# Cross attention and a gated feed-forward on one core: half-height score products for batch 1, whole-row stores of the state tokens, and a redrawn instruction order

## The chip, the cores and the metric

The kernel runs on 1 core of one Trainium2 chip. The metric is the device time of the program in microseconds (us). Three timed executions of the kernel before lie between 647.27 and 648.13 us, with a median of 647.93 us.

## The reference

There are B = 8 batches, H = 8 heads, S = 512 tokens and Ns = 32 state tokens of D = 64 elements per head. Tokens read the states and states read the tokens; all 8 x (512 + 32) result rows of 512 elements then go through a gated feed-forward with d_ff = 1536.

```python
scale = 1.0 / np.sqrt(D)
a = softmax(scale * x @ state.T)          # [B, H, 512, 32]
xread = a @ state                         # [B, H, 512, 64]
a2 = softmax(scale * state @ x.T)         # [B, H, 32, 512]
sread = a2 @ x                            # [B, H, 32, 64]
t = concatenate([xread, sread], axis=2)   # rows of 512 = all heads
out = ((t @ w_a) * (t @ w_b)) @ w_out
```

(The reference's softmax adds 1e-9 to its sum; it is written out there.)

## The kernel before

**Two parts per number.** Every fp32 operand of the large products is split into a rounded part and a remainder (names ending in `_h` and `_l`), and each product is three matmuls: h·h, l·h and h·l. ScalarE (ACT) makes the rounded part by a copy, VectorE (DVE) subtracts to get the remainder, and TensorE (PE) multiplies.

**Stages.** For tokens, `a @ state @ w_a` is computed as `a @ (state @ w_a)`: the small product of states and weights comes first, either directly (`Batch.direct0`, `Batch.direct`, lines 773 to 801) or by way of a scratch tensor in memory (`project`, `Batch.load`). `layer1` (line 922) multiplies it with the transposed attention weights `at_h`, `at_l` into the banks `ab`, and `layer2` (line 951) or `term` (line 1231, a scheme of seven products for pairs of batches) multiplies with the output weights into the banks `acc`. Finished token tiles are transposed by DVE and stored (`Batch.give`). The 8 x 32 state rows go last, as a unit of their own (`States`, line 859; `states2`, line 962): their sums stand in two `ms` banks, i = 0 and i = 1, of 128 rows each.

**Scores.** Batches 0 and 1 come first (`attend`, line 1010). `Attention.scores` (line 616) makes the scores of one batch and one of two groups g of four heads. The input holds two heads side by side over 64 rows each, and the states are stored with zeros in the rows of the other head, so a product runs over all 128 rows (64 of them zeros) into 32 output rows: 4 products per group, 8 per batch. Batches 2 to 7 use another function, `scores` (line 545), with 64 rows of contraction, in which heads of both groups alternate. For batch 1 the scores are kept by two ACT copies (`keep`, line 633), transposed by PE (`turned`), reduced, exponentiated and normed by DVE and ACT, transposed back and split into `at_h`, `at_l`.

**The end.** In the last call of `states2`, tile i = 0 is copied out of its bank by ACT (`States.close`, line 904) and stored by two DMAs (`States.give`, line 910), one per half of the columns h. Tile i = 1 is copied before its last matmuls, which go into two fresh banks of 256 columns; DVE adds each of these to the copy and each half is stored by its own DMA. A half is not contiguous in a row of the output: it is 4 pieces of 64 elements (256 bytes) in each of 128 rows.

**Order.** All calls are first recorded as units (one instruction, or several that belong together), and then issued in the order of a written-out list, `ORDER` (line 142). Each engine works through its own units in that order, and so does the queue of SyncE (SP), which issues every DMA. The list has 4896 units: 2556 of PE, 1035 of DVE, 734 of ACT and 571 of SP.

Of the kernel before, what the change touches and what calls it, by code (L numbers as in the profile page):

```python
# [14 lines left out]
ALU = mybir.AluOpType  # L15
# [4 lines left out]
P = 128  # L20
# [122 lines left out]
6 40-42 1 12-13 54 7 3 0 23 14 43-45 55 46-48 56 28 49 8-9 2 15 68 24 50 29 10 4 57 25-26 58 115 16 30 59 51 31 60 33  # L143
17 61 52 75 20 18 69 34 114 21 116 62-63 37 82 38 53 35 22 64 712 70 77 381 538 117 65 530 66 202 19 83 118-120 67 71
714 36 84 88 212 217 299 85-86 72 89 87 121 128 122 94 90 207 123 91 73 92-93 104-106 129 95 107 124 130 96 125 108
131 382 98 132 99 126 222 100 133 158 127 134 97 39 101-102 76 213 78 214 164 161-162 165 109 103 135 167 166 110 159
136 111 215 139 137 142 140 79 204 366 168 376 138 141 300 163 148-149 554 203 702 150-151 143 563 144-145 713 209 112
160 205 80 223 152 146 208 153 539 147 186 194 190 169 187 113 371 198 191 219 722 154-155 170 210 199 218 195 224 171
156 715 386 176 172 229 220 196 173 236 200 177 157 178 174 197 201 179 225 692 378 260 239 175 704 237 180 192 368
181 263 555 182 247 562 248 377 240 564 264 367 238 188 703 540 383 393 301 211 183 241 249 732 546 242 250 369 384 27  # L150
717 243 716 251 244 189 245-246 266 304 302 265 267 252-253 261-262 705 32 184 373 388 724 607 254 275-278 269 723 270
379 305 271 279 372 193 185 272 280 291 531 273 374 541 556 274 303 387 257 281 268 255 400 297 230 375 258 231 292
226 259 403 306 282 307 389 707 293 725 334 395 335 401 308 390 328 309 916 310 74 404 402 311 547 604 336 391 288 565
608 289 698 285 232 318 283 312 733 337 256 718 294 726 708 727 313 338-339 548 314 566 227 346 568 295 569 315 233
316 585 405 693 317 606 329 406 330 290 319 570 298 296 407 234 408-409 411 532 5 412 325 358 410 331 587 286-287 824
533 326 417 586 385 332 719 605 720 577 284 567 709 340 359 734 341 413 342 588 414 343-344 327 590 415 578 735 416
360 571 589 345 721 814 572 81 461-462 354 380 322-323 464 737 347 324 418 728 463 333 350 433-434 534 394 465 362 351
435 596 436 579 437 355 729 557 439 396 438 710 597 609 363-364 320 440 361 321 348 598 580 445 441 352 356 365 424
442 466 694 558 549 467 706 421 443-444 419 695 425 357 353 528 430 730 629 422 468 599 469 610 581 446 472 559 535
699 470 630 397 631 582 426 634 420 473 349 427 452 474 423 428 431 471 432 453 475 573 478 612 429 476 449 632 494  # L160
611 834 550 583 206 542 600 455 711 477 529 495 615 479 748 458 731 456 744-745 459 496 450 497 613 447 460 454 451
221 398 491 536 633 498 614 500 457 482 816 483 480 649 484-485 640 501 551 746 749 448 742 492 502 648 503 601 486
621 602 543 743 747 488 493 552 739 622 499 510-511 641 487 504 804 740 603 522 228 1224 906 506 1225 741 505 514 1227
523 1243 584 560 399 524 481 489 507 512 515 490 1226 1228 759 508 758 513 1244 696 518 1245 642 736 697 1229 519 235
516 700 1230 1246 520 1247 517 525 635 1200 825 1248 1257 664 1255 643 1231 760 544 1232 1260 1233 1201 1258 561 1202
11 1203 521 644 1204 738 1205 1249 1194 1261 826 623 1234 1250 553 1218 526 665 1195 624 1197 1241 1235-1236 509 625
1237 756 537 1214 1251-1253 757 1259 1238 626 645 216 761 627 1219 1254 1239 768 1256 545 1240 797 666 1215 1242 769
646 754 370 936 1196 805 1198 1262 1199 628 1216 651 1263 765 815 667 527 755 647 1268 1264 668 827 1375 1220 1376 616
1210 650 836 750 817 1265 751-752 669 652 753 764 1206 806 1207 1266 1269-1271 766 1267 767 1211 1272-1273 1208 1274
658 1290 1209 1282-1283 1399 1284 670 1377 671 1275-1277 1221 762 1278-1279 1285 1293 653 1217 1294 1286 807 1280 1291  # L170
1281 1287 772 1379 763 1288 1295 1292 818 1289 679 835 809 770 654 1296 701 591 1297-1298 673 907 1299 672 1301 1300
392 1302 773 1223 1303 771 828 819 1304-1305 837 1400 1440 829 1382 1307 1306 1323 1308 926 1212 1315 820 574 808 1380
1316 1309 674 659 656 1310-1311 831 1312-1314 918 1317 1442 1324 1318-1319 1213 832 821 1326 1401 1445 1320-1321
1334-1335 782 1383 811 838 1325 1322 1327 1336-1337 830 1328 833 1446 784 927 1329 1378 783 675 1330-1333 822 1356
1443 1222 1340 678 1338 799 655 812 1357 917 1339 1441 1342 1358 839 1384 1343 1444 660 1344 810 1345 1359 1341 1447
774 1348 661 1480 1349 1346 841 1350 1347 813 1499 1351 1462 775 919 1352 1354 785 1467 1353 846 1361-1362 1409 1360
1464 1363 847 842 938 937 778 676 592 780 1402 662 1364 1355 939 1406 908 840 677 1365 686 781 1367 1381 663 1368 1366
657 928 844 1410 779 1483 680 1369 1373 1562 909 786 1503 1370 776 845 1371-1372 777 1385 681 788 1421 843 687 1374
1391-1392 789 911 688 1386 1403 1387 1407 1422 1393 1388 910 1394 823 1389 1404 912 1395 1390 1396 1468 1481 1512 1423
# [3 lines left out]
1565 1439 1476 894 1451 1472 1500 1454 862 1419 858 1477 691 1455-1456 1452 873 1453 1471 865 793 859 1415 1554 1457  # L183
1420 876 1478 1460 1458-1459 1479 860 878 921 1504 1485 1416 1486 1556 1473 1487-1488 879 1501 1461 874 893 1509 1489
1474 1491-1492 1490 877 922-923 1566 1581 1475 1557 948 1493 861 1494 1497 900 1505 875 1495-1496 1506 1525 1539 884
1517 1510 866 1555 932 1498 1502 1559 1526 1679 1511 946 1531-1532 933 684 885 1558 1564 994 867 1514 895 940 1527
1533 1528 924 1522 1534 1507 1529 864 934 1540 1680 1530 1523 1560 925 1561 1583 949 1518 863 888 943 1508 996 947
1543 1775 1582 935 1584 995 1537 1519 794 950 1524 1520 1535-1536 1521 1544 1567-1568 1622 1538 951-952 1585 795 889
997 1569 956 953 962 954 1570-1573 963 1152 1613 1574-1576 944 964 1603 998 1546 1586 1605 796 1587 965 1542 1625 901
1547 1588 945 1579 1714 801 1604 1606 1545 942 999 1623 1645 1577-1578 1580 1548 1589 1550 1590 1655 1591-1593 1609  # L190
1594-1597 1610 802 1598 1551 1715 955 1552 1614 1601 1549 1599 1626 1600 880 957 1001 1656 1627 1616 803 1000 1628
1624 1611 1541 1553 881 896 1602 960 1619 1615 1617 1739 967 1633 1612 902 1153 1629 882 887 1634 636 1607 1630 961
1620-1621 1631 897 1154 1632 1608 886 1155 1635 1166 1636 1647 1618 1738 958 1681 1651 1648 1637 1654 903 1639 1652
# [3 lines left out]
1812 1694 1708 1702-1703 1157 1704-1705 1744 1720 1745 1712 1709 1724-1725 1710 1726 1717 1004 1660 1168 1756 982 1711  # L197
1741 1727 973 1005 1776 1169 1713 980 1175 1742 1757 1730 1162 1728 1731 1759 1891 1787 1006 1732 1729 1746 1733 1736
1159 1743 1721 1786 1718 1163 1851 1835 1760 1758 1761 983 1894 1753 1734 1754 1762 1719 1735 1737 1763 891 1722
# [160 lines left out]
def attn_moe(ctx, tc, xt, xn, sd, wl, w_out, out):  # L360
# [238 lines left out]
    class Attention:  # L599
# [776 lines left out]
```

## Time and profile before

| what | value |
|---|---|
| median of 3 timed runs | 647.93 us |
| the profiled execution's own time | 650.51 us |
| its span (first to last instruction) | 648.7 us |
| PE, DVE, ACT busy share of the span | 98%, 86%, 63% |
| granted TensorE clock, mean over the span | 0.995 |
| memory read, written | 119.80 MB, 55.05 MB |

The profiled execution is 2.58 us over the median of the timed runs; 1.8 us of its own time lie outside the span. Busy time of PE includes the pipelining of matmuls, so a busy share of 98% says that there was always a matmul under way, not that they followed each other at the smallest distance.

### The profile page before, as it was taken

Reading aid. Unit: us, or ns where it says so; the run is one execution under the profiler, and the core shown is the slowest. Engines: PE = TensorE matmul, PEld = TensorE weight load, DVE = VectorE, ACT = ScalarE, POOL = GpSimd, SP = SyncE. Lnnn points to the kernel's source line nnn. Section 1 sums busy time; section 2 is a strip of 40 time slices with the busy share of each in tenths; the row PEclk is TensorE's granted clock in tenths of the full one; section 3 lists DMA queues with packets and bytes.
Section 4 is the critical chain, followed back from the end, with each engine's and each line's share of the span. In section 5 each row is a group of like instructions: output and inputs, shape, how many; then the busy total and the mean of one; then the engine's idle time right before and its main releaser. Section 6 shows DMA issues by size and latency. Waiting matters only on the chain.

```text
span 648.7 us, 10343 instructions
## 1 busy us (share of the span) xinstructions
PE 636.4 (98%) x3554; PEld 496.8 (77%) x3554; DVE 557.4 (86%) x1035; ACT 407.2 (63%) x751; POOL 0.7 (0%) x6
## 2 busy tenths in 40 slices
PE   7999999999999999999999999999999999999996
PEld 4666777667887887786878886888788888888885
DVE  4799999998996898999998999999976887476785
ACT  3889886799994667657666765664443834544331
POOL 0000000000000000000000000000000000000000
PEclk9899999999999999999999999999999999999999
DMA  8998888999699989999979789977998366387706
GB/s 308 311 405 275 277 275 284 355 303 368 223 340 316 335 306 326 303 343 260 307 273 352 238 285 358 302 253 218 292 294 246 104 198 216 97 264 218 232 1 162
DMA packets 145380, 175.54 MB, mean 271 GB/s; under 512 B 48048, under 2 KB 102832, under 8 KB 145328
## 3 DMA queue, kind: packets, MB, share of 16 engines
q1 hardware_dynamic: 145328, 174.89, 82.6%
q8 instruction: 28, 0.46, 0.3%
q14 instruction: 24, 0.20, 0.1%
HBM read 119.80 MB, written 55.05 MB: 270 GB/s over the span
## 4 chain that ended last, share of the span: by engine, by line
PE 78%; DVE 11%; ACT 4%; DMA 4%; issue 2%; SPq 0%; DVEq 0%; POOLq 0%; POOL 0%; ACTq 0%
PE ab L1333 38%; PE acc L1333 30%; PE ms L1333 10%; DMA wt<-s_dram 2%; DVE kept_g L1333 2%; DVE g_l L1333 1%; DMA p_raw<-scr 1%; DVE stg L1333 1%; DVE s_p L1333 1%; DVE m L1333 1%; DVE p_l L1333 1%; DVE a_tr L1333 1%; DVE xst L1333 1%; ACT wq L1333 1%; DMA scr<-sw 1%
## 5 line engine op out<-in xcount | busy, mean ns | idle before, releaser
L1333 PE MATMUL acc<-g_h,wt 128*128 128x512 f32 x588 | 203.8, 392 | 0.5 <-DMA wt<-s_dram 0.5
L1333 PE MATMUL ab<-at_h,p_h 128*128 128x512 f32 x384 | 148.1, 398 | 2.3 <-ACT a_sb L1333 1.5
L1333 ACT COPY a_sb<-ab 128x512 f32<-128x512 f32 (+1 forms) x120 | 67.9, 566 | 130.9 <-PE ab L1333 120.3
L1333 PE MATMUL ab<-at_l,p_h 128*128 128x512 f32 x384 | 146.8, 391 | 0.1
L1333 PE MATMUL ab<-at_h,p_l 128*128 128x512 f32 x384 | 145.0, 392 | 0.0
L1333 PEld LDWEIGHTS acc<-g_h,wt 128*128 128x128 f32 x588 | 109.8, 188 | 27.3 <-issue 3.4
L1333 PE MATMUL acc<-g_l,wt 128*128 128x512 f32 x294 | 108.5, 390 | 0.0
L1333 PEld LDWEIGHTS ab<-at_h,p_h 128*128 128x128 f32 x384 | 72.2, 188 | 27.7 <-ACT a_sb L1333 7.5
L1333 ACT CAST g_h<-kept_g 128x512 fp32r<-128x512 f32 x126 | 76.8, 622 | 20.8 <-DVE kept_g L1333 11.2
L1333 DVE TENSOR_TENSOR g_l<-kept_g,g_h 128x512 fp32r<-128x512 f32 x126 | 84.3, 681 | 5.6 <-PE acc L1333 2.8
L1333 DVE TENSOR_TENSOR kept_g<-ab,a_sb 128x512 f32<-128x512 f32 x84 | 57.6, 686 | 32.5 <-PE ab L1333 25.3
L1333 PEld LDWEIGHTS ab<-at_h,p_l 128*128 128x128 f32 x384 | 72.1, 188 | 16.6 <-issue 1.7
L1333 PEld LDWEIGHTS ab<-at_l,p_h 128*128 128x128 f32 x384 | 72.1, 188 | 15.1 <-DVE at_l L1333 0.5
L1333 PEld LDWEIGHTS acc<-g_l,wt 128*128 128x128 f32 x294 | 55.2, 188 | 11.2
L1333 DVE TENSOR_TENSOR stg<-acc,stg 128x512 f32<-128x512 f32 x82 | 55.4, 683 | 7.2 <-PE acc L1333 5.3
L1333 ACT CAST p_h<-p_raw 128x512 fp32r<-128x512 f32 x72 | 44.3, 621 | 12.4 <-DMA p_raw<-scr 11.3
L1333 DVE TENSOR_TENSOR p_l<-p_raw,p_h 128x512 fp32r<-128x512 f32 x72 | 48.4, 680 | 3.7 <-ACT p_h L1333 3.7
L1333 PE MATMUL ab<-xs,sw_st 128*128 128x512 f32 (+1 forms) x192 | 51.1, 337 | 0.4 <-ACT a_sb L1333 0.4
L1333 ACT COPY sw<-ms 128x512 f32<-128x512 f32 x72 | 41.4, 589 | 11.4 <-PE ms L1333 10.9
L1333 PEld LDWEIGHTS ab<-xs,sw_st 128*128 128x128 f32 x192 | 34.5, 188 | 7.7 <-ACT a_sb L1333 1.2
L1333 PE MATMUL acc<-g_h,wo 128*128 128x512 f32 x96 | 33.3, 396 | 0.0
L1333 DVE TENSOR_TENSOR kept_g<-kept_g 128x512 f32<-128x512 f32 x42 | 28.4, 679 | 0.1
(130 smaller groups left out, 817.9 us busy)
## 6 DMA issues: line engine op xcount, KB each, us to landing
wt<-s_dram SPq DMA_DIRECT2D x42, 512.0 KB, 6.1
scr<-sw SPq DMA_DIRECT2D x72, 256.0 KB, 5.3
p_raw<-scr SPq DMA_DIRECT2D x36, 512.0 KB, 5.8
wt<-wo_dram SPq DMA_DIRECT2D x63, 256.0 KB, 5.0
raw<-wl SPq DMA_DIRECT2D x24, 512.0 KB, 7.1
x_in<-f_dram SPq DMA_DIRECT2D x36, 256.0 KB, 4.5
out<-turned SPq DMA_DIRECT2D x64, 128.0 KB, 4.4
xn<-xn SPq DMA_DIRECT2D x16, 512.0 KB, 5.3
```

The costliest lines, as they stand in the source:

```text
L1333: getattr(obj, method)(*map(real, args), **{k: real(x) for k, x in kw.items()})
```

## The change

Three things change.

1. Batch 1's scores: the 8 products of 128 rows become 8 products of 64 rows, with the heads of the two groups alternating. They stay one unit of the list.
2. States' output: each of the two tiles is stored by one DMA of 128 rows of 2,048 contiguous bytes, where there were two of 512 pieces of 256 bytes each. For tile i = 1 the DMA comes after both additions. The program has two units fewer (4894), both of them DMAs.
3. The list `ORDER`: all of its 200 lines are replaced. The first seven PE units are the same; after them the order differs on every engine, from beginning to end.

```diff
         def scores(self, psp, tag):
...
             self.raw = kept[self.b][:, self.g]
+            if self.b:
+                return
             with rec.together():
                 self.unread(0, self.s)
...
+        def product(self, hp, hh):
+            n = at(self.g, 2 * hp + hh) * NS
+            nc.tensor.matmul(self.s[n:n + NS], lhsT=self.st[ROWS[hh], hp, hh * NS:(hh + 1) * NS], rhs=self.x[ROWS[hh], hp], start=True, stop=True)
...
-        def give(self, i, h, ps=None):
-            o = self.sums[:, i].rearrange("p (j k x) -> p j k x", j=4, x=32)[:, :, 2 * h:2 * h + 2]
-            if ps is not None:
-                v = o.rearrange("p j k x -> p k j x")
-                nc.vector.tensor_tensor(out=v, in0=ps.rearrange("p (k j x) -> p k j x", k=2, x=32), in1=v, op=ALU.add)
+        def add(self, i, h, ps):
+            v = self.sums[:, i].rearrange("p (j k x) -> p k j x", j=4, x=32)[:, 2 * h:2 * h + 2]
+            nc.vector.tensor_tensor(out=v, in0=ps.rearrange("p (k j x) -> p k j x", k=2, x=32), in1=v, op=ALU.add)
+
+        def give(self, i):
             r = B * S + i * P
-            nc.sync.dma_start(out=out[r:r + P].rearrange("p (j k x) -> p j k x", j=4, x=32)[:, :, 2 * h:2 * h + 2].rearrange("p j k x -> p j (k x)"),
-                              in_=o.rearrange("p j k x -> p j (k x)"))
+            nc.sync.dma_start(out=out[r:r + P], in_=self.sums[:, i])
...
                 if last and i:
-                    u.give(i, h, ps)
-            if last and not i:
-                u.close(i)
-                for h in range(2):
-                    u.give(i, h)
+                    u.add(i, h, ps)
+            if last:
+                if not i:
+                    u.close(i)
+                u.give(i)
...
             for a in gs:
                 a.load()
+            for a in gs:
+                a.scores(*ms)
             with rec.together():
-                for a in gs:
-                    a.scores(*ms)
+                for hp in range(2):
+                    for a in gs:
+                        for hh in range(2):
+                            a.product(hp, hh)
```

Of the list, the two lines before and after in which the scores of batch 1 stand (117 is their unit; 118 and 119 are the two ACT copies, 120 the PE transposes; 39 and 72 are ACT casts, 21 and 83 to 85 PE products, 73 and 546 DVE units):

```diff
-17 61 52 75 20 18 69 34 114 21 116 62-63 37 82 38 53 35 22 64 712 70 77 381 538 117 65 530 66 202 19 83 118-120 67 71
-714 36 84 88 212 217 299 85-86 72 89 87 121 128 122 94 90 207 123 91 73 92-93 104-106 129 95 107 124 130 96 125 108
...
+59 70 33 60 115 20 114 61 116 34 217 300 18 52 37 82 702 53 62 83 63 19 38 77 530 212 35 64 69 202 65 71 117 538 39
+84-85 21 72 66 118-119 371 73 67 120 546 88 121 128 86 207 22 87 122 89 36 90 712 222 94 376 129 76 91-93 104-105 123
```

## Rows read from the trace of the kernel before

**Rows 1.** The page: busy time and share by engine, then the chain by engine.

```profile
PE 636.4 (98%) x3554; PEld 496.8 (77%) x3554; DVE 557.4 (86%) x1035; ACT 407.2 (63%) x751; POOL 0.7 (0%) x6
...
PE 78%; DVE 11%; ACT 4%; DMA 4%; issue 2%; SPq 0%; DVEq 0%; POOLq 0%; POOL 0%; ACTq 0%
```

**Rows 2.** Windows: stretch; length, busy PE, PEld, DVE, ACT, POOL; clock; DMA; GB/s.

```profile
60.00:120.00 60.00, 59.91 (x345) 44.41 (x345) 58.78 (x121) 45.65 (x84) 0.00 (x0) 1.00 0.86 290
120.00:200.00 80.00, 79.68 (x378) 61.33 (x378) 70.61 (x131) 70.80 (x128) 0.00 (x0) 1.00 0.91 317
200.00:320.00 120.00, 118.02 (x535) 93.52 (x534) 109.29 (x195) 81.85 (x150) 0.00 (x0) 1.00 0.96 311
320.00:400.00 80.00, 79.55 (x595) 63.73 (x594) 75.34 (x138) 51.27 (x93) 0.00 (x0) 1.00 0.88 298
400.00:500.00 100.00, 99.60 (x690) 79.63 (x690) 89.91 (x173) 51.02 (x97) 0.00 (x0) 1.00 0.89 269
```

**Rows 3.** Chain, 21 to 26 us and at 58.8 us: start, length, work.

```profile
21.93 1.85 PE ms L1333 x16
...
24.45 0.87 PE ms L1333 x8
...
58.76 1.02 PE ms L1333 x16
```

**Rows 4.** Timeline, ACT, 21.9 to 26 us: start, length, instruction, [idle before].

```profile
21.96 0.59 ACT L1333 CAST at_h<-ab 128x512 fp32r<-128x512 f32 x1 [0.73 <-PE ab L1333]
...
22.99 0.59 ACT L1333 COPY kept<-ms 128x512 f32<-128x512 f32 x1
23.85 0.59 ACT L1333 COPY kept<-ms 128x512 f32<-128x512 f32 x1 [0.28 <-PE ms L1333]
...
25.29 0.64 ACT L1333 CAST wo<-t 128x512 fp32r<-128x512 f32 x1
```

**Rows 5.** Timeline, DVE, 22 to 27 us.

```profile
22.55 0.47 DVE L1333 TENSOR_SCALAR t<-raw 128x512 int32<-128x512 uint32 x1 [1.23 <-DMA raw<-wl]
24.92 1.29 DVE L1333 TENSOR_REDUCE m<-ms 128x16 f32<-128x512 f32 x2 [1.91 <-PE ms L1333]
...
26.72 0.68 DVE L1333 TENSOR_TENSOR wo<-t,wo 128x512 fp32r<-128x512 f32 x1
```

**Rows 6.** Timeline, PE: batch 1's scores (21.86 us on), batch 2's (58.69 us on).

```profile
21.86 1.06 PE L1333 MATMUL ms<-x_raw 128*32 128x512 f32 x8
22.74 1.04 PE L1333 MATMUL ms<-xg 128*32 128x512 f32 x8
...
58.69 0.62 PE L1333 MATMUL ms<-x_raw 64*32 64x512 f32 x2
...
58.73 0.62 PE L1333 MATMUL ms<-x_nat,s_p 64*32 64x512 f32 x2
59.14 0.60 PE L1333 MATMUL ms<-x_raw 64*32 64x512 f32 x2
```

**Rows 7.** Timeline, the end: the last DMA issues (SPq), last matmul, additions (DVE).

```profile
643.02 2.65 SPq L1333 DMA_DIRECT2D out<-sums  x4
...
643.48 0.28 PE L1333 MATMUL acc<-wo_st,g_l 128*128 128x256 f32 x1
643.70 0.75 DVE L1333 TENSOR_TENSOR sums<-acc,sums 128x256 f32<-128x256 f32 x2 [2.10 <-ACT sums L1333]
...
645.09 0.58 SPq L1333 DMA_DIRECT2D out<-sums  x1
```

**Rows 8.** Page, DMA issues: count, KB each, median us from issue to landing.

```profile
out<-sums SPq DMA_DIRECT2D x4, 128.0 KB, 2.2
```

**Rows 9.** Tile x_raw, only its first DMA (576 KB, at 0.7 us).

```profile
L1333 SPq DMA_DIRECT2D x_raw<-xt x1: 406/406/406, 0.7 to 0.7; - x1
...
DMA to landing us min/median/max: 3.5/3.5/3.5
```

**Rows 10.** Chain, its longest wait for a DMA: start, length, work.

```profile
192.61 7.94 DMA p_raw<-scr
```

More of the change, by code (lines that the diff above doesn't have):

```diff
@@ L148 @@
[L148 to L152, printed above, removed]
@@ new lines @@
+2033 2091 1032 2306 2083 1027 2307 2081 2062 2578 2084 2096 2067 2097 2063 2059 2085 2125 2585 2094 2086 2088 2064
+2239 2072 1029 2111 2240 2087 2060 1050 2098 1060 2061 2308 2210 2103 2285 2100 2202 2104 2112 2089 1035 2117 2260
+1033 2201 2099 2259 2068-2070 1042 2073 2118 1061 2286 2203 1049 2113 2119 2074 2114 2309 1030 2071 1058 2101 2115
+2167 1040 2168 2075 2238 2120 2116 2294 2426 2121 1043 1041 2123 2204 2122 2128 2124 2438 2102 1028 1051 2205 2187
+2129 2105 2169-2170 2188-2189 2131 1031 2406 2148 2429 2178 2171 2179 2132 2193-2194 2172 1048 2190 1068 2195 2133
@@ new lines @@
+2337 2398 2342 2399 2343 2403 2344 2166 2186 2507 1086 1067 2417 2345 2432 2400 2411-2412 2435 2257 2353 2433 2413
+2434 2418 1070 2404 2371 2354 2401 2480 2419 2444 2414 2436 2445 1087 2370 2437 2448 2420 2415 2446 2508 2481 2449
+2482 2176 2421 2483 2447 2571 2405 2416 2485 1088 2422 2361 2465 2486 2484 2423 2457 1075 2372 2569 2362 2374 2450
+1084 2424 2509 2529 2154 2175 2363 2183 1076 2373 1077 2451 2510 2487 1085 2364 2586 2452-2454 2256 2458 2466 2549
+2455 2380-2381 2459 2512 2460 2456 2365 2461 2513 1090 1078 1096 2470 2382 2570 1079 2511 1091 2531 2463 2472 2532
@@ new lines @@
+2844 2840-2841 2771 2376 2778-2779 2842 2935 1123 2819 2849 2916 2845-2846 2856 2780 2859 2751 2772 2860 3007 2748
+2847 2853 1135 2966 2857 2848 2861 2854 2862 2588 2863 2923 1125 2755 2815 2858 2377 1121 2864 2855 2823 1136 1126
+2753 2592 2828 2920 2850 2871 2938-2939 2865 2921 2745 2953 3178 2866 2816 2867 2749 2824 1137 2868 2378 2752 2940
+2869 2746 2956 2870 2825 2747 2826 2138 2922 2917 2937 2967 2957 1124 2872 3008 2941 2978 2590 2942-2943 1142 2918
+2829 2827 2737 2979 2781 2589 2830 2929 2950 2831 2359 2919 1127 2980 2930 1138 2754 1143 2962 2158 2954 3034 2924
@@ new lines @@
+2944-2945 2738 1146 2931 2925 2992 1139 3016 2963 1140 2959 2742 2981 2741 2946 2379 2932 2982 2969 2926 2947 3230
+2948 3075 2680 2983 3129 1141 3009 3171 2927 3010 2949 2990 2970 2984 2756 3035 2996 2985-2986 3017 2960 3019 3205
+3011 2951 2987 2928 3306 3066 2971 2958 3020 3056 3012-3013 2993 3273 2997 3283 2360 2139 3284 3078 3186 3021-3023
+2760 2964 3239 2761 3266 2988 1151 3036 2968 2961 2975 3014 2995 2757-2759 2763 3037 3079 2976 2762 3076 3024 2989
+3025 3039 3032 2764 2972 3095 3206 2973 1147 2991 3038 3040 2876 2974 3042 3077 2879 3043 1144 2896 3187 3044 3189
@@ new lines @@
+3026-3027 3067 3041 3057 3045 3028 2897 2977 3058 3130 3059 3128 3046 3229 3062 3060 2877 3047 2998-2999 3029 2880
+3054 3000 2901 3030 3061 3031 3001 3048-3049 2878 2994 2882 1148 3003 3033 2898 3063 3172 3004 2899 3050 3005-3006
+3064 3080 3096 3051 3081 3052 3240 3082 3068 3002 3083-3084 3053 3131 2883 3055 3085 3065 1150 3282 3173 3086 3092
+3094 3087 3188 3174 3069 1149 3088 2671 3089 2881 3090 2900 3091 3269 3104 3072 3114 3073 3070 1145 3115-3116 3175
+3074 3271 3522 3117 3151 2902 3231 3176 3100 3093 3103 3101 2884 3238 3190 3180 3308 3177 3247 3120-3122 3307 3118
@@ new lines @@
+2907 3119 3332 3183 3126 3132 3295 3123 3184 3411 3153 3124-3125 2908 3340 3071 3152 3097 3105 3127 3250 3309
+3197-3198 3098-3099 3106-3107 3191 3102 3181 3108 3134 3192 3179 2903 3185 3110 3251 3193 3182 3330 3194 3133 3248
+3111 3296 3199 2888 3112 3109 3195 3331 2909 3211 3459 2889 3272 3196 3156 2885 2904 3207 3200 3208 3212 3201 3462
+3203 3268 3213 3297 3371 3232 3412 3157 3113 3215 3274 3216 3249 2776 3217 3393 3209 3202 3218-3219 2905 3214 3235
+3233 3220 3137 3227 3234 3313 3241 2248 3236 3158 3252 3204 3253 3210 3237 3352 3221 2890-2891 3285 3277 3244 3280
@@ new lines @@
+3351 3523 3416-3417 3425 3148 3438 3289 3838 3418-3419 3515 3408 3420 3346 3421 3403 3476 3426 3404 3435 3469
+3427-3428 3434 3167 3465 3405 3500 3470 3525 3575 3491 3612 3492 3409 3429 3493 3441 3471 3485 3494-3495 3294 3410
+3149-3150 3432 3442 3549 3347 3486 3496 3406 3293 3487-3488 3168 3519 3447 3477 3489-3490 3436 3524 3466 3169 3448
+3520 4221 3445 3516 3482 3287 3497 3795 3467 3517 3503 3527-3528 3468 3680 3504 3529 3619 3572 3290 3530 3475 3521
+3638 3478 3450 3479 3526 3480 3554 3550 3483 3498 3531 3455 3518 3456 3484 3533-3534 3551 3453 3288 3532 3481 3510
@@ new lines @@
+3748 3754 3840 3917 3755 3729 3875 2674 3815 3727 3730 3734 3792 3731-3732 3756 3896 3763 3704 3733 3599 3764 3814
+3735 3876 3757 3765-3766 3781-3782 3788 3767 3898 3769 3768 3770 3738 4031 3864 3895 3937 2775 3878 3771 3793 3740
+3970 4087 3772 3739 3741 3958 3794 4035 3837 3773 4190 3775 3800 3774 3776 3801 3706 3789 3802 3971 3803-3804 3879
+4012 3905 3805 3849 3790 2682 3812 3968 3742 3877 4044 3850 3880 3806 3899 4149 3807-3808 3816 3809 3900 3918
+3810-3811 3851 3826 3813 3852 4218 2784 3707 3853-3854 3791 3841 3855 3842 3856 4124 3901-3902 3843 3903 2247 3868
@@ new lines @@
+3844 3959 3845-3846 3827-3828 3847 3858 3848 3860 4295 3857 3907 3869 3881 4115 3904 3708 3817 4125 4045 3887 4219
+3882-3884 3818 2683 3920 3829 3913 3885 3888-3889 3886 3921 4089 3890 3914 4049 3891 3893 3892 2785 3922 3919
+3923-3924 3894 3819 3758 3909 4075 3925 3941-3942 3926 3859 4015 3944 4116 3927 3945 3820 4034 3946 3934 3947-3948
+4088 3928 3949 4013 3956 3908 3938 4090 3929-3931 3943 3932 3939 3950 3933 4014 3951 3963 3861 3940 4002 3862 3952
+3935 3915 4016 3953-3954 3980-3981 3960 3955 3982-3983 4032 3984 3865 3985-3986 3910 3987 3866 3957 3989 3972 3863
@@ new lines @@
+4814 4725 4744 4822 4745 4815 4604 4726 4816 4775 4749 4746 4758 4787 4750 4759 4782 4823 4817 4824 4783 4760 4818
+4751 4761 4819 4620 4770 4784 4771 4825 4797 3762 4826-4827 4772 4752 4779 4621 4828 4780 4841 4693 4753 4829-4830
+4842 4781 4843 4798 4831 4788 4799 4757 4762 4832 4789 4755 4849 4844 4850 4833 4790 4851 4623 4852 4696 3752
+4845-4846 4853 4800 4754 4854 4801 4791 4855 4765 4697 4847 4856 4834 4698 4624 4865 4848 4699 4766 4764 4858 4756
+4700-4701 4802 4804 4694 4866 4792 4857 4860 4868 4867 4869 4859 4861-4862 4803 4794 4870 4872-4874 4879-4880 4793
@@ L343 @@
+4795 4863 4763 4881 4796 4875 4805 4876-4877 4885 4889 4882 4886 4890-4891 4884 4883 4892 4887-4888 4893
 """
```

321 lines of the change are left out of this document (137 added, 184 removed), and 19 rows, old and new, of the table ORDER.

## The prediction

> **What bounds the kernel now.** I read the page first. TensorE is under way in 98% of the span, VectorE in 86%, ScalarE in 63%, and the chain that ended last runs through TensorE for 78% and through VectorE for 11% [rows 1]. Busy time of TensorE can hide small gaps, so I looked at the windows next: from 60 to 500 us TensorE lacks 0.09, 0.32, 1.98, 0.45 and 0.40 us, together 3.24 us, at the full clock [rows 2]. So there the time is matmul work, which the change leaves as it is, plus at most 3.24 us of holes. VectorE is close behind in the first part: 58.78 of 60 us from 60 to 120 us [rows 2]. That leaves three places where time can move: the start, where engines still wait for each other; the holes; and the end, where TensorE's last matmul ends at 643.76 us [rows 7] and the span at 648.7 us.
>
> **1. Batch 1's scores.** They stand in the chain with 1.85 us, 16 records, two per fp32 product [rows 3]. The first group's eight begin at 21.86 us and the second's at 22.74 us [rows 6]: four products side by side, in four rounds of about 0.45 us. Batch 2's scores are 16 records as well, written as the change writes batch 1's, and take 1.02 us in the chain [rows 3]: eight begin between 58.69 and 58.74 us, the other eight from 59.14 us [rows 6], two rounds and a margin for changing the form. TensorE's part therefore falls by 1.85 - 1.02 = 0.83 us. What lies behind it: two ScalarE copies of 0.59 us, of which the second had to wait for the second group until 23.85 us [rows 4], then transposes of 0.87 us [rows 3], then VectorE, idle for 1.91 us until they came [rows 5]. What reaches the end of the program lies between a loss of 0.5 us (rival A, below, with nothing to fill the wait) and a gain of 0.83 us. I take 0.83 us, because the redrawn list also gives the idle VectorE work it needs later: it puts a row maximum (unit 546, about 0.65 us by the two of 1.29 us) and a subtraction (unit 73, 0.68 us) ahead of batch 1's maxima and takes a conversion of 0.47 us (unit 714) from there [rows 5]. That is 0.86 us of VectorE work brought forward, about what TensorE wins, and from 60 to 120 us the two engines are bound together [rows 2].
>
> In batch 2's scores, two products of one group with different row halves go into one bank, and still eight start within 0.05 us of each other [rows 6]. The Trainium skill, page "TensorEngine Tiling (Array Packing)", section "Restrictions and Gotchas", says that different row tiles cannot access the same PSUM bank at once. By that rule the pairs would go one after the other and this term would be 0, for a sum of 647.3 us; the trace disagrees with it for the very same pattern (rival D).
>
> **2. States' output.** Now four DMAs are issued one behind the other from 643.02 us, 2.65 us in all; VectorE's additions end at 643.70 + 0.75 = 644.45 us, but the last issue begins only at 645.09 us, since the queue is still busy with the one before [rows 7]. With one DMA per tile, the first is issued at 643.02 us as now and is through long before 644.45 us, and the last is issued when the additions are done, at about 644.5 us: 0.59 us earlier. It carries 256 KB rather than 128 KB. No row shows a lone store of 256 KB. The nearest are the same stores with 128 KB, 2.2 us from issue to landing [rows 8], and a lone load of 576 KB at the start, 3.5 us, whose issue takes 0.41 us against 0.58 us [rows 7, 9]. The landing may thus take from 0.2 us less (the shorter issue of plain rows) to 1.3 us more (as much as 576 KB), so this term lies between a gain of 0.8 us and a loss of 0.7 us. I take the 2.2 us of the same tensor, which is much nearer in size: a gain of 0.59 us. Two DMA issues of about 0.66 us each go from the queue [rows 7]; nothing else waits behind them.
>
> **3. The list.** It is redrawn from end to end, not in the first part alone. Counted from the two lists, TensorE's units are displaced by 6 places on average (6 x 0.22 us = 1.3 us; 118.02 us for 535 records from 200 to 320 us [rows 2]), ScalarE's by 6, VectorE's by 7 and the DMA queue's by 8, at most 66. No instruction is added or removed, so its price is what it does to holes. It can give back no more than the 3.24 us that are there [rows 2]; a loss has no end in the trace, and I bound it by as much again. Counts of positions show no side: the loads stand about as far ahead of their readers as before. I take 0 and keep both ends. In the first seven TensorE units nothing changes, and VectorE's first work merely moves from one idle stretch to another; I cost that at nothing, covered by the wait for the first scores, and at 0.47 us, one conversion [rows 5], if that cover is gone.
>
> **The sum.** 0.83 + 0.59 + 0 = 1.42 us. The profiled execution took 650.51 us, so another would take 649.1 us with a span of 647.3 us. The timed runs have a median 2.58 us lower, 647.93 us; against it the forecast is 646.5 us. A measurement of this kernel can tell about 0.2%, 1.3 us, from no change, so the sum lies just at the edge of what can be seen.
>
> **Rival A: the scores' gain is waited away.** In the new list two casts (units 39 and 72, 0.59 and 0.64 us) stand on ScalarE between the cast of `at_h` and the two copies of the scores. That cast ends at 21.96 + 0.59 = 22.55 us; the copies then run from 23.78 to 24.96 us, where now the second ends at 23.85 + 0.59 = 24.44 us [rows 4]. The transposes would end 0.5 us later than now although the products end 0.8 us earlier. For it: ScalarE is the only reader of these banks. Against it: TensorE has products (84, 85, 21, 66) to fill the wait, and ScalarE is less loaded afterwards. Only the end's 0.59 us stay: 647.3 us, within 0.2%.
>
> **Rival B: the new list also closes holes.** Half of the 3.24 us, for instance by issuing earlier a load like the one on which the chain stands for 7.94 us [rows 10]: 646.5 - 1.6 = 644.9 us. For it: 1.98 of the 3.24 us lie in one stretch, 200 to 320 us, with the DMA engines busy at 0.96 [rows 2], and a few better placed loads would do. Against it: that stretch has no DMA time to spare.
>
> **Rival C: the new list opens holes, slower.** The place is the same DMA queue between 190 and 340 us. It issues strictly in order, so a store that waits for its data holds up each load behind it; eight places are about nine microseconds of queue (569 DMAs in 649 us), more than such a load may come late without stopping the products that read it. If the holes double, 3.24 us are added: 646.5 + 3.2 = 649.7 us. It decides from 2.7 us of new holes on (649.2 us). For it: DMA is at 0.96 there and the chain already runs through loads [rows 2, 10]. Against it: TensorE has work of several independent kinds to put in front.
>
> **Rival D: two row halves of one bank go one after the other.** Batch 1's products then need four rounds of 0.45 us again, 1.85 us, and the first term is 0: 647.3 us. This is the rule of the Trainium skill, page "TensorEngine Tiling (Array Packing)", section "Restrictions and Gotchas", as in part 1. For it: nothing in batch 1's own rows, which have no row halves. Against it: two rounds for batch 2 [rows 6].
>
> **How the numbers follow.** The forecast's case (both gains, holes within 0.8 us of now) has 0.30, and reaches from 645.7 to 647.3 us; 0.18 of it lie below 646.6 us, the edge of 0.2%. Rival B has 0.27, all faster. Rival A has 0.20 and rival D 0.03, both no change. Rival C has 0.20: slower. Faster 0.18 + 0.27 = 0.45; same 0.12 + 0.23 = 0.35; slower 0.20. The range of 8 in 10 leaves out B's lower part (from four fifths of the holes on: 646.5 - 2.6 = 643.9 us) and the worse half of C (from 649.3 us on, just past where it decides): 643.9 to 649.3 us. As no change and faster share most of it, the likeliest case's own range stands above.
>
> **What would show it.** Right: batch 1's scores in about 1.0 us on TensorE, two rounds of eight; two stores of the states' sums, the last issued about 0.05 us after the additions and landing about 2.2 us later, so that 4.3 us lie between TensorE's end and the span's end instead of 4.9 us; busy time of TensorE lacking again some 3 us between 60 and 500 us. Rival A: the second copy of the scores ends after 24.4 us and the first long run of `ab` products begins no earlier than 25.3 us. B and C: the lack in the windows well under or over 3.24 us. The prediction is wrong if the end does not come nearer to TensorE's last matmul, or if holes of over 1 us appear between 60 and 200 us, where 0.41 us is lacking now.

## The result, and the profile after

The changed kernel takes 655.0 us (median of nine runs); the kernel before took 647.3 us beside it. The ratio is 1.0089, 95% interval 1.0064 to 1.0114: slower by 0.9%, and 5.7 us above the upper end of the range. The ratios here leave out times that fell in the chip's slower state (661.50 us of these nine, 664.34 us in e12) and are not the quotient of the two medians, which would be 1.012. In the profiled executions the span went from 648.7 to 653.6 us.

The page, busy time and the chain by engine, as in [rows 1]:

```profile
PE 637.7 (98%) x3554; PEld 496.7 (76%) x3554; DVE 559.8 (86%) x1035; ACT 408.1 (62%) x751; POOL 0.7 (0%) x6
...
PE 83%; DMA 7%; DVE 5%; issue 1%; SPq 1%; ACT 1%; DVEq 0%; POOLq 0%; POOL 0%; ACTq 0%
```

The page hides the loss: TensorE is again under way in 98% of the span. Only the chain has moved, from 11% VectorE and 4% DMA to 5% and 7%. The windows of [rows 2] say more (stretch; length, busy PE, PEld, DVE, ACT, POOL; clock; DMA; GB/s):

```profile
60.00:120.00 60.00, 60.00 (x346) 44.85 (x345) 58.46 (x122) 48.28 (x87) 0.00 (x0) 1.00 0.91 307
120.00:200.00 80.00, 79.62 (x379) 61.25 (x378) 71.96 (x132) 71.80 (x132) 0.00 (x0) 1.00 0.96 331
200.00:320.00 120.00, 116.25 (x522) 90.90 (x521) 105.97 (x188) 77.16 (x142) 0.00 (x0) 1.00 0.93 294
320.00:400.00 80.00, 77.29 (x576) 60.65 (x576) 71.95 (x132) 49.29 (x88) 0.00 (x0) 0.98 0.87 282
400.00:500.00 100.00, 99.35 (x689) 79.58 (x688) 91.51 (x178) 52.34 (x101) 0.00 (x0) 1.00 0.88 275
```

TensorE lacks 0, 0.38, 3.75, 2.71 and 0.65 us, 7.49 together, where it was 3.24. Two stretches carry the difference: 200 to 320 us, and 320 to 400 us, where the clock also falls below 1.00. Up to 200 us nothing more is lost.

**The first loss, 240 to 305 us.** SP's DMA issues and its waits (us in total, times, longest), then the chain, then VectorE's and TensorE's timelines, all in that stretch:

```profile
225.77 0.38 SPq L1342 DMA_DIRECT2D at_l<-a_dram  x1
231.68 0.37 SPq L1342 DMA_DIRECT2D s_dram<-ws_l  x1
...
237.49 0.45 SPq L1342 DMA_DIRECT2D s_dram<-ws_h  x1
241.53 0.53 SPq L1342 DMA_DIRECT2D x_in<-f_dram  x1
```

```profile
SPq L1342 <- DMA s_dram<-ws_l: 5.7, 2, 3.5
SPq L1342 <- DVE ws_l L1342: 5.5, 1, 5.5
```

```profile
243.23 6.52 DMA scr<-sw
```

```profile
249.84 0.69 DVE L1342 TENSOR_TENSOR wq<-x_in,t 128x512 fp32r<-128x512 f32 x1 [3.04 <-DMA scr<-sw]
```

```profile
252.39 0.50 PE L1342 MATMUL ab<-at_h,p_h 128*128 128x512 f32 x1 [1.71 <-DVE kept_g L1342]
```

They are read from top to bottom. SP issues nothing from 226.15 to 231.68 us and from 237.94 to 241.53 us: in its fixed order it stands before an issue that is not ready (for 5.5 us it waits for VectorE's `ws_l`, for 3.5 us for the landing of a store), and all behind it stand too. The store `scr<-sw`, issued at 243.23 us, then lands at 249.75 us. VectorE's `wq` step waits 3.04 us for it. The step reads nothing that the store writes; what it can need is the buffer that the store gives back (this is argued, no view names buffers). Behind it on VectorE stands `kept_g`, and TensorE stands for 1.71 us until that comes. From 225 to 300 us VectorE waits twice for `scr<-sw`, 5.0 us in all. The DMA engines, busy at 0.96 from 200 to 320 us in before [rows 2], are less busy in two stretches now:

```profile
230.00:240.00 10.00, 10.00 (x44) 7.67 (x43) 8.95 (x15) 5.81 (x11) 0.00 (x0) 1.00 0.87 265
250.00:260.00 10.00, 8.05 (x34) 5.99 (x34) 9.97 (x17) 7.98 (x15) 0.00 (x0) 1.00 0.84 268
```

A halt of SP and a hole in the use of the DMA engines are not yet the loss, though. In before SP stands for 5.0 and 3.8 us around the same place, and in e1 (below, the old list with both edits) for 4.7 and 5.9 us, with a hole as deep, and TensorE lacks nothing in these two windows (it lacks 0.96 us between them, 0.8 us of it a wait for ScalarE):

```profile
230.00:240.00 10.00, 10.00 (x45) 7.97 (x43) 8.39 (x14) 4.44 (x9) 0.00 (x0) 1.00 0.82 281
250.00:260.00 10.00, 10.00 (x45) 8.02 (x44) 8.92 (x16) 9.21 (x17) 0.00 (x0) 1.00 1.08 385
```

What tells the lists apart is VectorE's wait. From 222 to 300 us it never waits for `scr<-sw` in the seven traces with the old order there (before, e1, e3, e4, e6, e7, e9), and for 4.1 to 5.0 us in the four with the new order as it is (the changed kernel, e2, e5, e11).

**The second loss, 385 to 393 us.** TensorE's timeline at the second reading of the states (64 products of 64 columns, 128 records), and the instruction queue in the DMA view from 386.4 to 386.6 us:

```profile
384.76 1.92 PE L1342 MATMUL ms<-xn,a 128*32 128x64 f32 x121
388.73 0.32 PE L1342 MATMUL ms<-xn,a 128*32 128x64 f32 x7 [2.05 <-issue]
```

```profile
q8 instruction: 1, 0.02, 33.6%
```

After 121 of the 128, TensorE stands for 2.05 us, and no semaphore and no transfer of data is named ("issue"). Among what moves at that moment is one packet of the queue for instructions, 16 KB, from 386.43 us on (packets, MB, share of 16 engines). The whole program has 28 of them, on average some 254 recorded matmuls and weight loads (7,108 over 28) apart, and so by their number they carry TensorE's instructions. Behind the stop, the granted clock falls to the lower of its two levels, 1.2 instead of 2.4 GHz (windows, columns as above):

```profile
385.00:390.00 5.00, 2.95 (x131) 2.56 (x121) 4.15 (x9) 2.48 (x6) 0.00 (x0) 0.96 0.93 305
390.00:393.30 3.30, 3.30 (x10) 2.57 (x9) 3.21 (x9) 0.53 (x2) 0.00 (x0) 0.55 0.91 295
```

Nine matmuls of 128x512 take 3.64 us there (389.55 to 393.19 us), instead of 2.04 us at their usual spacing of 0.227 us. The stop and the lower clock are 2.05 + 1.60 = 3.65 us together.

**The start.** The chain, as in [rows 3], then the two groups on TensorE and the landing of one input (tile `xg`):

```profile
20.38 2.04 PE ms L1342 x16
...
23.55 0.87 PE ms L1342 x8
...
57.86 1.02 PE ms L1342 x16
```

```profile
20.31 1.05 PE L1342 MATMUL ms<-x_raw 64*32 64x512 f32 x4
21.35 0.62 PE L1342 MATMUL ms<-xg 64*32 64x512 f32 x2
```

```profile
L1342 SPq DMA_DIRECT2D xg<-xt x1: 1034/1034/1034, 16.1 to 16.1; - x1
...
DMA to landing us min/median/max: 5.1/5.1/5.1
```

The scores take 2.04 us instead of 1.85 [rows 3], but 1.04 us of that is a wait: `xg`, issued at 16.1 us, lands 5.1 us later at 21.2 us, and the products that read it start at 21.35 us. Four records had gone ahead from 20.31 us on.

A warning on comparing these two profiles: the execution of before ran at the lower clock early on, and the changed one did not.

```profile
14.00:21.00 7.00, 6.26 (x69) 2.78 (x51) 6.69 (x15) 4.65 (x9) 0.00 (x0) 0.51 0.64 230
```

That row is from before. Of the other runs of the old order, one shows it too (e6) and three do not (e1, e3, e4); those three are 1.1 to 1.5 us ahead of it by 28 us of the span. So most of the 2.1 us by which the changed kernel leads at 217 us is no merit of its list.

**The end**, as in [rows 7, 8] (SP, last matmuls, additions, then the landing of the stores):

```profile
649.11 1.89 SPq L1342 DMA_DIRECT2D out<-sums  x2
...
649.45 0.40 PE L1342 MATMUL acc<-wo_st,g_l 128*128 128x256 f32 x2
649.83 0.76 DVE L1342 TENSOR_TENSOR sums<-acc,sums 128x256 f32<-128x256 f32 x2 [2.07 <-ACT sums L1342]
```

```profile
DMA to landing us min/median/max: 2.0/2.1/2.2
```

The last store is issued at 650.6 us, as the additions end (649.83 + 0.76 = 650.59). From TensorE's end (649.85 us) to the end of the span are 3.77 us, where there were 4.98 and 4.3 were forecast.

A table worked out from the traces shows where the time goes. Every matmul is given its usual spacing (0.227 us for 128x512); the lag is the time at which a given amount of such work begins, less the work.

```
work done (us)          28     196     232     304     352     388     604
before               12.54   21.38   22.00   24.34   25.41   26.72   31.03
after                11.82   19.30   22.80   27.52   28.41   33.38   37.96
e1 (old list)        11.32   20.04   21.51   23.12   24.11   25.42   30.96
e7 (old stretch)     11.22   18.94   19.43   22.73   23.63   28.71   33.10
e11 (tiny matmuls)   11.98   19.26   22.41   27.83   28.52   29.97   34.06
```

Against e1, which has both edits and the old list, the changed kernel is 0.7 us ahead at 196, 4.4 us behind at 304 and 8.0 us behind at 388: some 5 us in the first place, 3.7 us in the second.

### The profile page after: what moved, and what is told of

The parts are those of the page before. It is cut to its first block, busy times and chain, and to the rows that moved or that the text cites. A ratio compares the mean times of both kernels' runs of the same rounds, so it can differ in the third digit from the quotient of the medians.

```text
span 653.6 us, 10309 instructions
## 1 busy us (share of the span) xinstructions
PE 637.7 (98%) x3554; PEld 496.7 (76%) x3554; DVE 559.8 (86%) x1035; ACT 408.1 (62%) x751; POOL 0.7 (0%) x6
## 4 chain that ended last, share of the span: by engine, by line
PE 83%; DMA 7%; DVE 5%; issue 1%; SPq 1%; ACT 1%; DVEq 0%; POOLq 0%; POOL 0%; ACTq 0%
PE ab L1342 40%; PE acc L1342 32%; PE ms L1342 11%; DMA wt<-s_dram 3%; DMA scr<-sw 3%; SPq L1342 1%; DVE kept_g L1342 1%; DMA xn<-xn 1%; DMA e_dram<-a_tr 1%; DVE s_p L1342 1%; DVE m L1342 1%; DVE p_raw L1342 0%; DVE stg L1342 0%; DVE g_l L1342 0%; DVE wq L1342 0%
## 5 line engine op out<-in xcount | busy, mean ns | idle before, releaser
L1342 PE MATMUL ab<-at_h,p_h 128*128 128x512 f32 x384 | 149.6, 401 | 4.1 <-DVE kept_g L1342 4.0
L1342 PE MATMUL acc<-g_l,wt 128*128 128x512 f32 x294 | 111.7, 392 | 0.1
```

Source lines behind the costliest of these rows:

```text
L1342: getattr(obj, method)(*map(real, args), **{k: real(x) for k, x in kw.items()})
```

## The experiments

Each ratio is to the kernel before on the same chip, with its 95% interval. Unit numbers are the list's own; up to 4883 they are the same in both lists.

**e1: the old list, both edits.**

```diff
-ORDER = (the new list)
+ORDER = (the list of before, numbers fitted; at its end the last store behind both additions:)
+... 4892 4887 4888 4893
```

> The order of before (the last output store put at the end, since it now needs both additions), with both edits: batch 1's scores with 64 rows and the states' output in one transfer per tile. Theory L, the new list lost the time (DMA waits between 225 and 300 us and a stall at 386 us) and the two edits gain: 0.83 us for the scores and 0.6 to 1.2 us for the output off 647.3, so 645.3 to 645.9. Theory E, the edits themselves cost (the 64-row scores come no faster and upset what follows): 650 or more. In between, 647.0 to 647.6, if the scores' gain is waited away and the output's is taken back.

Measured: 647.71 us beside 648.47, 0.9983 (0.9966 to 0.9999). So the edits gain a little (the interval just leaves out no change), and the list has lost the time.

**e2: the new list, neither edit.**

```diff
-            if self.b:
-                return
...
-            if last:
-                if not i:
-                    u.close(i)
-                u.give(i)
+                    u.give(i, h, ps)
+            if last and not i:
+                u.close(i)
+                for h in range(2):
+                    u.give(i, h)
...
-            for a in gs:
-                a.scores(*ms)
             with rec.together():
-                for hp in range(2):
-                    for a in gs:
-                        for hh in range(2):
-                            a.product(hp, hh)
+                for a in gs:
+                    a.scores(*ms)
```

> The new order with neither edit (the output's two extra stores put right behind the ones they were split from). Theory L: the whole loss and more, since the edits' gain is gone: 656 to 657.5, with the stall in the second reading of the states still there at about 386 us. Theory E: the time of before, 646.5 to 648.5.

Measured: 655.26 us, 1.0104 (1.0068 to 1.0141), just under the 656 us expected. In its trace the stop in the second reading is there again; the reading takes 5.2 us, and the lower clock follows from 389.6 us on. With e1 this settles that the list alone is slower by 1%.

**e3: the old list, the scores edit alone** (the diff of the scores as in the change, all else as before).

> The order of before with the scores edit alone. Forecast's first term: TensorE's time for batch 1's scores goes from 1.85 to about 1.03 us, since in before both of its input tiles had landed 1.4 us before the scores began, and the run is 646.3 to 646.7. Rival A, the gain is waited for elsewhere: 647.0 to 647.6. Rival D, the row halves do not run at once: the scores stay at 1.85 us or take 2.05, 647.2 to 647.6.

Measured: 647.73 us, 0.9987 (0.9969 to 1.0006): by the time alone, not clear of no change. TensorE's timeline:

```profile
19.95 0.62 PE L1343 MATMUL ms<-x_raw 64*32 64x512 f32 x2
20.22 0.62 PE L1343 MATMUL ms<-xg 64*32 64x512 f32 x2
20.23 0.62 PE L1343 MATMUL ms<-x_raw 64*32 64x512 f32 x2
20.25 0.62 PE L1343 MATMUL ms<-xg 64*32 64x512 f32 x2
```

Eight records begin within 0.3 us, and the next matmul begins at 21.23 us: 1.28 us for the scores, of which 0.27 pass until `xg`'s products start (it lands at 20.09). Other runs with the edit show 1.35 (e1), 1.27 (e5, e7, e12) and 1.13 us (e8); runs without it 1.85 each (e2, e4, e6). So the term is a gain of 0.5 to 0.7 us, when `xg` comes in time. Where it lands 0.45 to 1.0 us after the first products, the scores take 1.60 (e9), 1.68 (e11) and 2.17 us (e10).

**e4: the old list, the output edit alone** (the diff of the output as in the change, the last store put at the end of the list).

> The order of before with the output edit alone. From TensorE's last matmul to the end of the span: 4.98 us in before, 3.77 in the changed kernel. If that is the edit's doing, 646.0 to 646.7 here, with a tail of 3.6 to 4.0 us; if it was the new list's order of the last additions and stores, 647.0 to 647.6 and a tail of 4.8 to 5.1.

Measured: 647.09 us, 0.9974 (0.9955 to 0.9992). The end, and the stores' landing:

```profile
640.15 1.85 SPq L1336 DMA_DIRECT2D out<-sums  x2
...
640.61 0.28 PE L1336 MATMUL acc<-wo_st,g_l 128*128 128x256 f32 x1
640.84 0.76 DVE L1336 TENSOR_TENSOR sums<-acc,sums 128x256 f32<-128x256 f32 x2 [2.10 <-ACT sums L1336]
```

```profile
DMA to landing us min/median/max: 2.0/2.0/2.0
```

The tail is 4.06 us. Over the ten traces with this edit it is 3.73 to 4.18, over those without it 4.94 to 5.20 (e2, e3, e6 and before): about 1.0 us gained, in either list.

**e5: the second reading 11 matmuls later.**

```diff
-2984 2756 ...
+2984 ...
-... 3021-3023 2760
+... 3021-3023 2756 2760
```

> The changed kernel with one unit moved: the second reading of the states, 64 matmuls of 64 columns that TensorE issues in 2.0 us (256 instructions), put 11 matmuls later, right ahead of its first reader. In the changed kernel it began some 9 instructions after TensorE's code had crossed a block of 256 and stopped dead 2.05 us in its midst, while a 16 KB packet of the instruction queue came in, and the clock was at half for 3.4 us behind that; in before it began 35 instructions after such a crossing, the packet in hand. Theory C, it is the loading of code that stops TensorE: here the reading takes 2.0 us without a stop, no half clock behind it, and the run is 3.5 to 4.5 us under the changed kernel, 650.5 to 651.8. Theory W, it waits for something of its own (its input tiles, the row of matmuls behind it, a semaphore that the profile does not show): the stop comes again at the new place, and the time stays within 1 us of 655.0.

Measured: 652.9 us beside 649.12, 1.0051 (1.0039 to 1.0063), whose interval lies just under that of the changed kernel. The reading runs through:

```profile
386.88 1.99 PE L1342 MATMUL ms<-xn,a 128*32 128x64 f32 x128
```

No stop, clock 1.00 to the end. The packet of instructions had started at 383.7 us, 3.2 us ahead of the reading. The gain, 0.0038 or 2.5 us (give or take 1.8), is under the 3.5 us expected: the trace loses some 2 us elsewhere between 385 and 405 us.

**e6: the old list, the second reading 13 matmuls earlier.**

```diff
-2948 ... 2989 2928 2756 2360
+2756 2948 ... 2989 2928 2360
```

> The kernel before with one unit moved: the same second reading put 13 matmuls earlier, so that it begins some 9 instructions behind the crossing, as in the changed kernel, and after its last input tile has landed (0.6 us before by the trace of before). Theory C: the stop of about 2 us and the half clock appear in the old order, and the run is 2.5 to 4.5 us slower than before. Theory W: nothing stops there, or for under 0.6 us for the input tile, and the time is that of before within 1 us.

Measured: 650.93 us beside 649.12, 1.0023 (1.0010 to 1.0036). Slower, but not for the reason expected:

```profile
381.67 0.65 PE L1337 MATMUL ms<-xn,a 128*32 128x64 f32 x32
383.52 1.55 PE L1337 MATMUL ms<-xn,a 128*32 128x64 f32 x96 [1.19 <-DMA xn<-xn]
```

TensorE waits 1.19 us for an input tile after 32 records, and there is no stop of the other kind: the packet of instructions started at 381.13 us, ahead of the reading. This run decides nothing between the two theories. It does show that counting recorded matmuls doesn't say to the instruction where a block begins.

**e7: the old order in the stretch from 224 to 328 us.**

```diff
-ORDER = new
+ORDER = new[:1667] + sorted(new[1667:2443], key=old.index) + new[2443:]
```

> The changed kernel with the units of its list's places 1667 to 2443 (about 224 to 328 us) put back into the order that they have in before; all else as in the changed kernel. Theory Q, that stretch holds the loss of about 4 us of TensorE time (VectorE and the DMA queue wait for each other there): the lag that the changed kernel builds up against before between 240 and 305 us is gone, the stall at 385 us stays, and the run is 3 to 4.5 us under the changed kernel, 650.5 to 652. Rival: the loss comes from what the earlier part of the list leaves (a fuller queue, later inputs), and 1 us or less goes: 654 to 655.5.

Measured: 651.09 us beside 649.12, 1.0028 (1.0013 to 1.0042): 0.0061 under the changed kernel, 4.0 us (give or take 1.9). The windows, the first to be held against the changed kernel's 116.25:

```profile
200.00:320.00 120.00, 119.28 (x543) 95.24 (x542) 110.62 (x197) 80.58 (x147) 0.00 (x0) 1.00 0.94 300
320.00:400.00 80.00, 76.95 (x573) 60.31 (x573) 71.27 (x131) 47.98 (x87) 0.00 (x0) 0.98 0.90 290
```

TensorE lacks 0.72 us rather than 3.75, VectorE no longer waits for `scr<-sw` at all, and the DMA share is 0.98 from 230 to 240 us and 0.99 from 250 to 260. The second loss is untouched (3.05 us lacking, a stop of 2.11 us). The order of these 776 units made the first loss.

**e8: two stores earlier.**

```diff
-975 1019 ... 1008 1949 989 ... 988 2018
+975 989 988 1019 ... 1008 1949 ... 2018
```

> The changed kernel with two DMA issues moved: the two stores of one weight tile to DRAM scratch (scr<-sw, issued at 242.1 and 243.2 us and landing at 246.2 and 249.75) put right behind the copy that fills the tile, which is ahead of the two stores of batch weights that SP is held at from 238 to 241.5 us. VectorE's wq waited 3.0 us for the second of them, because it takes over the tile's buffer, with kept_g queued behind it and TensorE waiting 1.9 us. Theory Q: VectorE's wait for scr<-sw at 247 to 250 us is gone, TensorE's hole at 250 us too, and the run is 1 to 2.5 us under the changed kernel. Rival: the other transfers that are pushed back (x_in, p_raw, s_dram) are waited for instead, and the time is within 0.7 us of 655.

Measured: 654.16 us beside 649.12, 1.0068 (1.0048 to 1.0089). At 254 us of the span it is 3.2 us ahead of before where the changed kernel is 0.8 us behind; at 279 us nothing of the lead is left. VectorE's timeline:

```profile
258.33 0.43 DVE L1342 TENSOR_SCALAR t<-x_in 128x512 int32<-128x512 int32 x1 [2.44 <-DMA x_in<-f_dram]
```

So the named wait can be removed, and the next late transfer takes its place, as the rival had it. The whole time doesn't tell e8 from the changed kernel.

**e9: the mends of e5 and e7 together.**

> Both mends in one: the changed kernel with places 1667 to 2443 of its list in the order of before, and the second reading of the states put 11 matmuls later. If the two causes are separate and are all there is, their gains add: 1.0089 less 0.0061 (stretch) and 0.0038 (reading) against before, so a ratio of 0.998 to 1.000, the same as the old order with both edits (0.9983). If they overlap or something else was lost: 1.003 or more.

Measured: 650.09 us beside 649.26, 1.0018 (0.9999 to 1.0036). Both losses are gone from the trace: 119.92 of 120 us busy from 200 to 320 us, the reading in 2.0 us. The ratio falls by 0.0071 of the 0.0099 that were added up, and is 0.0035 above e1. The shortfall of 0.0028 is within the noise of the two differences; the 0.0035, some 2 us, is just outside it. Part of that shows in the trace: by the reckoning of the table above, the lag grows by some 3 us between 352 and 388 us of work in e9 and in e5, against 1.3 in e1 and 1.5 in e11. So moving the reading has a price of its own there; why was not tested.

**e10: only SP's issues of that stretch in the old order.**

```diff
-mid = new[1667:2443]
+mid = merge(PE, ACT, DVE units of new[1667:2443] in the new order, its SP units in the old order)
```

> The changed kernel with only SP's part of that stretch (its DMA issues of places 1667 to 2443) in the order of before; VectorE, ScalarE and TensorE keep the new order. Theory Q1, the order of the DMA issues made the loss: like the run with the whole stretch put back, a ratio to before of 1.002 to 1.004. Theory Q2, the order of the engines' own work made it (VectorE meets buffers that are not yet free): 1.007 to 1.010, with waits of VectorE for DMAs and of TensorE for VectorE's kept_g left in the stretch. Waits of engines for inputs that now come later than they are due would make it more than 1.010.

Measured: 658.17 us beside 649.26, 1.0140 (1.0112 to 1.0168). Slower still. One line of the trace:

```profile
253.12 0.79 PE L1343 MATMUL ab<-at_h,p_h 128*128 128x512 f32 x1 [2.33 <-DVE kept_g L1343]
```

The old order of the transfers doesn't suit the new order of the engines, and the clock falls here as well (0.52 from 252.8 to 256.3 us). Putting back the order of the issues alone doesn't remove the loss; the number doesn't prove the other theory either, since the mixture makes waits that neither list has.

**e11: the new list, 11 tiny matmuls more.**

```diff
             for _ in range(UNREAD.get((self.b, self.g), (0, 0))[k]):
                 nc.tensor.transpose(ps[:, :P], ident, ident)
+            for _ in range(11 if (self.b, self.g, k) == (0, 1, 0) else 0):
+                nc.tensor.matmul(ps[:32, :64], lhsT=ident[:, :32], rhs=ident[:, :64], start=True, stop=True)
```

> The changed kernel's list as it is, with 11 tiny matmuls (32 columns by 64) more among TensorE's opening dummy reads, into a tile that the next matmul writes anyway: 22 instructions more ahead of all that follows, some 0.2 us where TensorE waits for an input in any case. Nothing else is moved. Theory C, the stop at 385 us depends on where the second reading begins among the blocks of 256 instructions that TensorE's code is loaded in: now some 30 instructions behind the crossing as in before, the reading takes 2.0 us, no half clock follows, and the run is 1.5 to 4 us under the changed kernel: a ratio to before of 1.003 to 1.0066. Theory W, the stop belongs to the place in the list or to the time: it stays, and the ratio is 1.008 to 1.010.

Measured: 651.51 us beside 649.26, 1.0032 (1.0011 to 1.0053): adding work at 9 us took 3.7 us off the time, at 385 us.

```profile
385.32 1.99 PE L1344 MATMUL ms<-xn,a 128*32 128x64 f32 x128
```

The reading has its old place in the list, its old neighbours and inputs, and no stop; the packet of instructions started at 380.7 us, and the clock stays at 1.00. Only the count of TensorE's instructions ahead of it differs. That speaks against a wait of the reading's own. The timed runs agree: the mean granted clock is at most 0.997 in all nine of the changed kernel, and 0.999 or 1.0 in nine of the twelve of e11. (The 11 products moved it by 44 recorded instructions, twice the 22 expected, as an fp32 product stands with two matmuls; the other three readings moved as much and stayed at 2.0 us.) In all, the six profiled runs with the reading at the new list's place and count (the changed kernel, e2, e7, e8, e10, e12) have the stop, with the packet inside the reading; the three where place or count was shifted (e5, e9, e11) have neither. In the six, TensorE goes on 2.2 to 2.4 us after the packet has started, whether that is 1.1 us (e10, a stop of 1.57 us) or 2.4 us (e2, 2.93 us) after the reading's first matmul. Nowhere else in the 14 traces does TensorE stand for over 0.25 us after the first 30 us with "issue" as the cause.

**e12: two conversions later on VectorE.**

```diff
-1011 ... 1023 2039 ... 1022 ... 1024 ... 2108
+1011 ... 2039 ... 2108 1023 1022 1024
...
-1027 2307 ... 1029 ... 2240
+2307 ... 2240 1027 1029
```

> The changed kernel with two conversions of batch weights put later on VectorE: the step wq<-x_in,t that waited for the store scr<-sw at 247 to 250 us goes behind some eight VectorE steps more (with its two copies on ScalarE), and the step t<-x_in that waited at 261 us three steps later. What is read from DRAM and when stays as it is. If these in-order waits of VectorE, with kept_g queued behind them, are what TensorE loses by in the stretch: no wait of VectorE for scr<-sw of over 1 us between 245 and 265 us, no hole of TensorE at 250 and 262 us, and 1.5 to 3 us under the changed kernel, a ratio to before of 1.004 to 1.0065. If other buffers and inputs are late in their turn (as when the two stores were put earlier): 1.007 to 1.010.

Measured: 656.13 us beside 649.9, 1.0088 (1.0057 to 1.0118): no gain shown. VectorE's timeline:

```profile
250.98 0.69 DVE L1342 TENSOR_TENSOR kept_g<-ab,a_sb 128x512 f32<-128x512 f32 x1 [2.10 <-DMA scr<-sw]
263.16 0.43 DVE L1342 TENSOR_SCALAR t<-x_in 128x512 int32<-128x512 int32 x1 [2.67 <-DMA x_in<-f_dram]
```

With `wq` out of the way, the next taker of a buffer, `kept_g` itself, waits for the same store. The wait went with the late store and not with the step that met it.

## Why the prediction was wrong

**Part 3, the list, is the step that failed.** It was taken at 0 with an end of 3.24 us, as much again as the holes of before. By e1 against the changed kernel the list costs 1.0089 - 0.9983 = 0.0106, about 7 us. The bound had no mechanism behind it: the holes that a list leaves say nothing of those that another may open. "Counts of positions show no side" was of no use. Loads were counted against their readers, but not who waits for a store that must land first, nor which stores stand behind a halt of SP's queue. Rival B did not come either: TensorE lacks 7.49 us from 60 to 500 us, not under 3.24.

**Rival C had the right kind of mechanism and nearly the right place**, SP's queue from 190 to 340 us: the trace shows SP standing, a store late, VectorE waiting with `kept_g` behind it, TensorE waiting. But it had SP's halts hold up loads for TensorE; SP halts as long in before and e1, and it is a wait of VectorE for a store that comes with the new list. Its price, 3.24 us, was close to the 4.0 us that e7 gives back; as it was only the holes of before doubled, that is luck. That the stretch's order makes the loss is shown by e7. Which unit in it starts the loss stays open: e8 and e12 each took one wait away and found it again at the next step, and e10 only mixed in new waits.

**The second loss was in no rival.** The stop of 2.05 us and the lower clock behind it, 2.5 to 3.7 us by e5 and e11, come from where the reading lies in TensorE's stream of instructions. The forecast took the order of TensorE's units to matter only through data and buffers, and read the queue for instructions in no view, though the page has its line. Without this loss the time would have been about 652 us, still outside the range. That the place in the stream decides is shown by e5 and e11; that the stop is a wait for the packet is inferred from their times.

**Part 1, the scores: right mechanism, term too large.** 0.83 us was forecast; where `xg` is there the edit gives 0.5 to 0.7 us, since in most of these runs the first products, of `x_raw`, begin before `xg` has landed and the others then wait for it. In the changed kernel's profile it gives nothing, because `xg` lands at 21.2 us. Rival A did not come: the copies of the scores run from 22.46 us for 1.08 us, right behind the scores, with the cast of `wo` already done. Rival D did not come: eight records of both row halves begin within 0.3 us (e3). The Trainium skill, page "TensorEngine Tiling (Array Packing)", section "Restrictions and Gotchas", says that different row tiles cannot access the same PSUM bank at once; the trace disagrees. One after the other, the pairs of one bank would take the scores to 1.85 us; they took 1.28 us, 0.27 of it the wait for `xg`.

**Part 2, the output: right, term too small.** The last issue comes 0.57 us sooner after TensorE's end (0.77 us in e4, 1.34 in before), as forecast. To that come 0.2 us for the landing (2.0 us, where the upper end had feared 1.3 us more), and the rest (0.1 us in e4, 0.4 us in the changed kernel) lies behind the landing. The row of the same tensor at half the size was the better guide than the load of 576 KB.

**The sum of parts 1 and 2**, 1.42 us, stands beside 1.1 us for e1 (0.0017, interval 0.1 to 2.2 us). The old list with the edits, e1 or e4, is the only improvement on the kernel before that was found here.

## What to carry to other kernels

How far units move says little of what a reordering costs in a program with no slack: here places moved by six to eight on average and the list cost about 7 us. List for each in-order queue what blocks it, which stores stand behind that, and who must wait for those. A halt of the queue or a hole in its use is not a loss by itself (e1 has both); look for the engine that waits behind it. Where a burst of short matmuls follows, look at when the code for it is loaded; a few idle instructions earlier were worth 3.7 us here (e11).

## What was not expected of the hardware

- TensorE's instructions come in packets of 16 KB, 28 in this program, most of them 15 to 34 us apart. The second reading issues as many instructions as one packet holds in 2 us, and TensorE stood in its midst where the packet had not come before it began: 1.57, 2.05, 2.11, 2.30, 2.23 and 2.93 us in e10, the changed kernel, e7, e8, e12 and e2, with the packet starting 1.1, 1.7, 1.8, 1.9, 1.9 and 2.4 us after the reading's first matmul.
- A stop of about 2 us was followed by 3.4 us at the lower clock in five of the six runs that had it; in e10, where it was 1.57 us, the clock stayed up.
- Eleven matmuls more made a kernel of 655 us faster by 0.6% (e11).
